# Seven Strassen products in place of four tiles for the output of token block 7

## Chip, cores and metric

The kernel runs on one core of a Trainium2 chip. The metric is the device time of one execution in microseconds (us), the median of several runs. The profile is of one further execution; its span is counted from the first to the last instruction that the profiler saw.

## What is computed

Eight batches, eight heads, 576 rows of 64 values. Keys and values are averaged over groups of 8 rows, attention is a softmax over the 72 averaged keys, and the heads' results, put side by side, make x of 4608 tokens by 512. Then a maxout layer with three weights and an output weight:

```
k_p, v_p = means of k, v over groups of 8 rows
x = softmax(q @ k_p.T / 8) @ v_p            # 4608 x 512
h = max(x @ w1, x @ w2, x @ w3)             # 4608 x 768
out = h @ w_out                             # 4608 x 512, float32
```

## The kernel before

The kernel subtracts w1 from w2 and w3 once (`sub_w`), so that h = x@w1 + max(0, x@(w2-w1), x@(w3-w1)). The first part goes straight through to the output by a weight `wm` = w1@w_out. The output of a token is therefore one sum over 512 + 768 = 1280 rows: `xT` against `wm` (4 slices of 128 rows) and the maxout value `hT` against `wo_sb` (6 slices).

The 4608 tokens are cut into nine blocks of 512, numbered 0 to 8. Blocks 0 to 5 get their maxout values by plain matmuls (`hidden`, L346). Blocks 6 to 8 get them by seven Strassen products (`seven`): the sums of activations T1 to T4 are made by `fold_x` (`fold_t`, L598), those of weights beforehand, and each product is done for three groups of rows, a, b and c (L733, 4 matmuls of 256 columns each). ScalarE copies products out of PSUM (L739, L743), VectorE adds others (L711) and takes the maximum (`best`, L714), which writes rows of `hT`: the group's row g with product 3, its row g+3 with product 4.

The output of a block is done in one of two ways. `project` takes four tiles of 128 tokens; a tile is 4 matmuls of 512 columns with `wm` (L391) and 6 with `wo_sb` (L395) into one PSUM bank, a copy by ScalarE (L400) and two stores of 128 KB by SyncE's queue (L404). `out_seven` does a block by seven Strassen products over 256 columns: each product is 5 matmuls for each of two halves m of 128 tokens (L670). Its sums come from three places: of weights from `fold_out`, 20 GpSimd subtractions and additions handed out one by one between the products (L628), of x from `fold_x` again, of maxout values from `fold_h`. Before the change only block 8 goes this way.

The three Strassen blocks run in `weave`, where the program order of every engine is written out by hand in the string `ORDER`. `1a` is product 1 of group a of the next block that has not had it (so the first is block 6's, the third block 8's); `T` is `fold_x` of the next block; `F` is half a tile of `project`; `s70` is a piece of batch 7's scores and `v62` chunk 2 of batch 6's attention output, which VectorE normalises and a DMA transpose on SyncE's queue (L239) puts into `xT`; `k7` is batch 7's keys. After `weave` come the remaining half tiles, `out_seven` of block 8 in the order 1 1 2 2 6 6 7 5 5 7 3 3 4 4, and as the very last work one tile cut into two halves of 256 columns, so that the end has short copies and stores.

PSUM in this stage: tags `pa` (2 banks) for products 1, 6, 5, 3, `sc` (2) and `bc` (1) for products 2 and 7/4, `po` (1) for tiles, `val` (2 banks, one buffer) for attention output.

Of the kernel before, what the change touches and what calls it, by code (L numbers as in the profile page):

```python
# [10 lines left out]
ALU = mybir.AluOpType  # L11
# [3 lines left out]
def kernel(  # L15
# [11 lines left out]
    nc = tc.nc  # L27
# [14 lines left out]
    NG = 9  # L42
# [338 lines left out]
    def project(n):  # L381
        hT = hTs[n]
        for mm in range(4):
            m = 4 * n + mm
            last = m == TOK // 128 - 5
            osb = sb3.tile([128, C], F32, name="osb", tag="osb", bufs=5)
            for c in ((slice(0, C // 2), slice(C // 2, C)) if last else (slice(0, C),)):
                tag = PW if len(pools) < 3 else (PO, SC, PA)[max(0, m - (TOK // 128 - 7))]
                po = psum([128, c.stop - c.start], F32, name="po", tag=tag[0], bufs=tag[1])
                for kc in range(KCH):  # L390
                    nc.tensor.matmul(po, xT[:, kc, bass.ts(m, 128)], wm_sb[:, kc, c],  # L391
                                     start=(kc == 0), stop=False)
                yield
                for jc in (0, 3, 1, 4, 2, 5):
                    nc.tensor.matmul(po, hT[:, jc, bass.ts(mm, 128)], wo_sb[:, jc, c],  # L395
                                     start=False, stop=(jc == JCH - 1))
                if c.start:
                    nc.vector.tensor_copy(out=osb[:, c], in_=po)
                else:
                    nc.scalar.copy(out=osb[:, c], in_=po)  # L400
                for u in range(2):
                    b, g = divmod(2 * m + u, NG)
                    dst = out[S * b:S * b + S, :].rearrange("(r g) c -> r g c", g=NG)
                    (nc.scalar if last and u else nc.sync).dma_start(  # L404
                        out=dst[:, GS[g], c], in_=osb[64 * u:64 * u + 64, c])
            yield
# [186 lines left out]
    def turns(n):  # L593
        return (pad3 if n % 2 else pad)[:, 0:4]

    def fold_t(e, x, t):
        for i, a, b in ((0, x[1], x[0]), (1, x[3], t[0]), (2, x[3], x[1]), (3, x[2], t[1])):
            e.tensor_tensor(out=t[i], in0=a, in1=b, op=ALU.subtract)  # L598

    def fold_x(n):  # L600

        x, t = halves(n), turns(n)
        for part in ([slice(0, 1), slice(1, 2)] if n == LAST else [slice(0, 2)]):
            fold_t(nc.gpsimd if n == LAST else nc.vector,
                   {i: x[i][:, part] for i in x}, [t[:, i, part] for i in range(4)])
        return {f"T{i + 1}": t[:, i] for i in range(4)}

# [22 lines left out]

    def fold_h(n):

        th[n] = ld.tile([128, 4, JH, HALF], F16, name="th", tag="ktFalse")
        h = {i: hTs[n][:, JH * (i // 2):JH * (i // 2) + JH,
                       HALF * (i % 2):HALF * (i % 2) + HALF] for i in range(4)}
        fold_t(nc.vector, h, [th[n][:, i] for i in range(4)])

    def out_seven(n):

        o = sb2.tile([128, 2304], F32, name="ob", tag="et")[:, 0:2048].rearrange(  # L640
            "p (j m c) -> p j m c", j=2, m=2)
        lo, hi = slice(0, HALF), slice(HALF, C)
        banks, done = {}, set()

        def store(e, j, c):
            for u in range(2):
                b, g = divmod(2 * (4 * n + 2 * j) + u, NG)
                dst = out[S * b:S * b + S, :].rearrange("(r g) c -> r g c", g=NG)
                e.dma_start(out=dst[:, GS[g]:GS[g + 2] + 1:4, c],
                            in_=o[64 * u:64 * u + 64, j, :, c])  # L650

        def product(i, m):
            of = "B" if i == 2 else "C" if i in (4, 7) else "A"
            if i in FIRST:
                tag = {"A": PA, "B": SC, "C": BC if m == 0 else SC}[of]
                banks[of, m] = psum([128, 2, HALF], F32, name=f"o{of}", tag=tag[0],
                                    bufs=tag[1])
            p = banks[of, m][:, 0]
            za, zb = PRODUCTS[i]
            for r in range(5):  # L660
                c = slice(128 * m, 128 * m + 128)
                if isinstance(zb, str):
                    z = int(zb[1]) - 1
                    left = turns(n)[:, z, r, c] if r < 2 else th[n][:, z, r - 2, c]
                else:
                    at = HALF * (zb % 2) + 128 * m
                    left = (xT[:, 2 * (zb // 2) + r, NB * n + at:NB * n + at + 128] if r < 2
                            else hTs[n][:, JH * (zb // 2) + r - 2, at:at + 128])
                right = out_s(int(za[1]))[:, r] if isinstance(za, str) else out_w(za, r)
                nc.tensor.matmul(p, left, right, start=(i in FIRST and r == 0), stop=(r == 4),  # L670
                                 skip_group_check=True)
            done.add((i, m))

            def copy(j, c):
                nc.scalar.copy(out=o[:, j, m, c], in_=p)

            def plus(j, c, p):
                nc.vector.tensor_tensor(out=o[:, j, m, c], in0=o[:, j, m, c], in1=p,
                                        op=ALU.add)

            if i in (1, 5, 6, 3):
                copy(i in (5, 3), lo if i in (1, 3) else hi)
            elif i == 2:
                plus(0, lo, p)
                if m:
                    store(nc.gpsimd, 0, lo)
            elif i == 4:
                plus(0, hi, p)
                if m:
                    store(nc.sync, 0, hi)  # L690
            if i in (5, 7) and (12 - i, m) in done:
                plus(1, hi, banks["C", m][:, 0])
            if i in (5, 7, 3) and all((z, m) in done for z in (5, 7, 3) for m in range(2)):
                store(nc.sync, 1, slice(0, C))

        return product

    def seven(n):
# [19 lines left out]
        def product(i, g):  # L718
            if i == 0:
                x.update(fold_x(n))  # L720
                return
            if not done:
                hTs[n] = new_hT()
            of = "B" if i == 2 else "C" if i in (4, 7) else "A"
            if i in FIRST:
                tag = {"A": PA, "B": SC, "C": BC}[of]
                banks[of, g] = psum([128, 2, HALF], F32, name=f"p{of}", tag=tag[0],
                                    bufs=tag[1])
            p = banks[of, g]
            for w in range(2):  # L730
                a, b = sw[w + 1][PRODUCTS[i][0]], x[PRODUCTS[i][1]]
                for kc in range(2):
                    mm = nc.tensor.matmul(p[:, w], a[:, kc, bass.ts(g, 128)], b[:, kc, :],  # L733
                                          start=(i in FIRST and w + kc == 0),
                                          stop=(w + kc == 2), skip_group_check=True)
            mms.append(mm)
            done.add((i, g))
            if i in (1, 6, 5):
                nc.scalar.copy(out=kept(i, g), in_=p)  # L739
            if i == 2:  # L740
                plus(top(g)[:, 0], 1, g, p)
            elif i == 3:
                nc.scalar.copy(out=top(g)[:, 1], in_=p)  # L743
                best(g, top(g))
            elif i == 4:
                plus(low[:, 0], 6, g, p)
                best(g + JH, low)
            elif i in (5, 7) and (12 - i, g) in done:
                plus(low[:, 1], 5, g, banks["C", g])
# [1 line left out]
        return product  # L751

    ORDER = """
        k7 F F T v62 1a 1b F s70 s71 6a 6b 2a 7a s72 v63 5a s73 F 2b 5b 4a s74 3a
        s75 F s76 7b 1c s77 v64 s78 4b 6c F v70 2c 5c 7c 3b F v71 3c F 4c 1a 1b T F
        v72 2b F 2a 6b 6a 7a F v73 5a F v74 3a 5b 4a F 1c F 6c 7b 3b T F 5c 4b F 7c
        1a 2c 2a 4c 6a 3c F 5a 7a 1b 2b 3a 6b 4a 1c 2c 5b 6c 7b 3b F 4b 5c F 7c 3c F
        4c
    """

    def weave():

        products, seen, sums = {}, {}, fold_out()
        for name in ORDER.split():
            if name == "F":
                next(tiles)
            elif name[0] in "ksvx":
                b = int(name[1])
                do(b, name[0] + name[2:])
# [20 lines left out]
    for n in range(2, 5):  # L790
# [8 lines left out]
    stage.close()  # L799
    pools.append(ctx.enter_context(tc.tile_pool(name="psq", bufs=1, space=PSUM,  # L800
                                                reuse_waits="tile")))
    tiles = (t for n in range(5, LAST) for t in project(n))
    weave()
    next(tiles)
    next(tiles)
    outs = out_seven(LAST)
    fold_h(LAST)
    for i, m in ((1, 0), (1, 1), (2, 0), (2, 1), (6, 0), (6, 1), (7, 0), (5, 0), (5, 1),
# [34 lines left out]
```

The softmax here doesn't subtract the row's maximum and nothing guards it: scores larger than these inputs give would overflow.

## Time and profile before

| what | before |
|---|---|
| time, median of 3 | 231.08 us (230.59 to 231.42) |
| span of the profiled execution | 229.0 us |
| TensorE busy | 219.8 us (96%) |
| VectorE busy | 130.5 us (57%) |
| ScalarE busy | 122.6 us (54%) |
| GpSimd busy | 140.0 us (61%) |
| a Strassen product of L733 (4 matmuls) | 0.44 us in the chain |
| a tile: L391 and L395 | 0.86 + 1.29 us in the chain |
| a product of `out_seven`, both halves (10 matmuls) | 1.09 us in the chain |
| VectorE: L711 / L714 | 685 / 810 ns mean, 18 each after 160 us |
| ScalarE: L739, L743 / L400 | 587, 584 / 585 ns |
| GpSimd sum of 128x256: L628, L598 | 668 to 921 ns by form |

The profile is read as follows. The chain of waits follows the work back from the last instruction: where it stays on one engine, that engine was never waiting, and its work sets the time. The windows give the busy time of every engine in a stretch. The timeline gives instructions in order of time with the idle time before them and what ended it. "xT<-xn" means that the instruction writes tile xT from tile xn.

### The profile page before, as it was taken

To read this page: it belongs to the slowest core of one execution; us is meant where nothing else is said; L and a number is where in the kernel's file an instruction comes from. 1 tells how busy PE (TensorE), PEld (TensorE's weight loads), DVE (VectorE), ACT (ScalarE), POOL (GpSimd) and SP (SyncE) were. 2 spreads that over 40 slices of the span, in tenths; PEclk is the share of its full clock that TensorE was granted. 3 is DMA by queue.
4 is the path that set the end of the run, shared out by engine and by line. 5 is a ranking of instruction groups with operands and counts; after the bars stand their busy time and mean duration, and the time that the engine had idled before them with its cause. 6 is when DMAs were issued, how large, how long until landed. Compare 5 with 4: busy or idle time off the path is not lost.

```text
span 229.0 us, 4411 instructions
## 1 busy us (share of the span) xinstructions
PE 219.8 (96%) x1686; PEld 134.9 (59%) x1687; DVE 130.5 (57%) x246; ACT 122.6 (54%) x221; POOL 140.0 (61%) x115
## 2 busy tenths in 40 slices
PE   7888999999999999999999999999999999999992
PEld 2477645568655545544554455455677667786682
DVE  3668876048426423632363236368578887897830
ACT  2277425756864586238623852683776435465330
POOL 7975201999959999999999759900343443920020
PEclk9999999999999999999999999999999999999999
DMA  6999999999569999986998799941421534301326
GB/s 172 208 197 197 211 202 208 194 177 225 106 110 216 221 161 212 159 194 119 223 153 199 127 218 189 190 110 24 92 53 40 121 71 87 84 11 46 76 68 183
DMA packets 47157, 33.52 MB, mean 146 GB/s; under 512 B 27104, under 2 KB 41888, under 8 KB 47136
## 3 DMA queue, kind: packets, MB, share of 16 engines
q0 software_dynamic: 16944, 16.98, 46.0%
q1 hardware_dynamic: 30032, 16.13, 32.2%
q8 instruction: 13, 0.21, 0.4%
q10 hardware_dynamic: 160, 0.13, 0.2%
q14 instruction: 8, 0.07, 0.1%
HBM read 34.60 MB, written 9.44 MB: 192 GB/s over the span
## 4 chain that ended last, share of the span: by engine, by line
PE 88%; DVE 6%; ACT 3%; issue 2%; DVEq 0%; ACTq 0%
PE pw L346 23%; PE po L395 18%; PE po L391 11%; PE pA L733 7%; PE psc L207 6%; PE pav L255 4%; PE pC L733 3%; PE wm L413 3%; PE pm L333 2%; PE oA L670 2%; PE pB L733 2%; DVE kz L198 2%; PE pqt L182 2%; DVE xn L263 2%; ACT kz L198 2%
## 5 line engine op out<-in xcount | busy, mean ns | idle before, releaser
L346 PE MATMUL pw<-xT,mw 128*128 128x512 f16 (+1 forms) x336 | 73.1, 349 | 0.4 <-ACT xT L249 0.2
L395 PE MATMUL po<-mwo,hT 128*128 128x512 f16 (+1 forms) x198 | 46.8, 373 | 0.0
L354 DVE TENSOR_TENSOR hT<-t,pw 128x512 f16<-128x512 f16 (+1 forms) x42 | 25.5, 610 | 36.7 <-ACT et L212 22.3
L346 PEld LDWEIGHTS <-mw 128*128 128x128 f16 x336 | 31.6, 98 | 21.5 <-DVE mw L319 0.6
L400 ACT COPY osb<-po 128x512 f32<-128x512 f32 (+1 forms) x32 | 18.5, 579 | 41.2 <-PE po L395 41.1
L212 ACT ACTIVATE et<-psc 72x576 f16<-72x576 f32 (+2 forms) x54 | 35.2, 660 | 7.1 <-PE psc L207 6.9
L151 POOL TENSOR_TENSOR half<-vt 72x2048 f32<-72x2048 f16 x7 | 28.4, 4060 | 14.1 <-DMA vt<-in_v_dram 13.7
L391 PE MATMUL po<-wm,xT 128*128 128x512 f16 (+1 forms) x132 | 33.0, 372 | 0.3 <-ACT osb L400 0.3
L352 ACT ACTIVATE t<-pw 128x512 f16<-128x512 f32 (+1 forms) x42 | 22.5, 537 | 13.4 <-PE pw L346 11.6
L263 DVE TENSOR_TENSOR xn<-pav,rcp 128x512 f16<-128x512 f32 x40 | 27.7, 691 | 1.6 <-DVE rcp L261 0.2
L395 PEld LDWEIGHTS <-hT 128*128 128x128 f16 x198 | 18.5, 98 | 16.3
L152 POOL TENSOR_TENSOR half<-half 72x1024 f32<-72x1024 f32 (+1 forms) x13 | 27.3, 2097 | 1.0
L207 PE MATMUL psc<-qT,kz 128*128 128x320 bf16 (+2 forms) x120 | 22.9, 278 | 1.8 <-DVE qT L184 0.9
L207 PEld LDWEIGHTS <-kz 128*128 128x128 bf16 x143 | 13.1, 98 | 14.7 <-ACT kz L198 2.0
L151 POOL TENSOR_TENSOR half<-ktFalse 96x1536 f32<-96x1536 f16 x6 | 18.6, 3099 | 4.3 <-DMA ktFalse<-in_k_dram 4.1
L255 PEld LDWEIGHTS <-et 72*128 72x128 f16 x320 | 15.4, 98 | 7.6 <-issue 0.3
L739 ACT CAST pad<-pA 128x512 f16<-128x512 f32 x27 | 15.3, 587 | 8.4 <-PE pA L733 6.0
L261 DVE RECIPROCAL rcp<-pav 128x8 f32<-128x8 f32 x40 | 8.2, 206 | 18.1 <-PE pav L255 17.9
L391 PEld LDWEIGHTS <-xT 128*128 128x128 f16 x132 | 12.1, 98 | 9.4 <-issue 0.4
L255 PE MATMUL pav<-vp,et 72*128 72x65 f16 x320 | 17.0, 194 | 0.1
L714 DVE SCALAR_TENSOR_TENSOR hT<-pad 128x512 f16<-128x512 f16 x18 | 14.4, 810 | 1.8 <-ACT pad L743 1.4
L733 PEld LDWEIGHTS <-sw 128*128 128x128 f16 x144 | 13.7, 98 | 2.7
(106 smaller groups left out, 279.2 us busy)
## 6 DMA issues: line engine op xcount, KB each, us to landing
out_dram<-osb SPq DMA_DIRECT2D x62, 128.0 KB, 3.2
ktFalse<-in_k_dram POOLq DMA_DIRECT2D x7, 576.0 KB, 6.6
qb<-in_q_dram POOLq DMA_DIRECT2D x7, 576.0 KB, 13.2
vt<-in_v_dram POOLq DMA_DIRECT2D x7, 576.0 KB, 10.9
mw<-in_moe_w_dram POOLq DMA_DIRECT2D x9, 256.0 KB, 9.2
ktTrue<-in_k_dram SPq DMA_DIRECT2D x3, 384.0 KB, 5.0
mwo<-in_moe_w_out_dram POOLq DMA_DIRECT2D x1, 768.0 KB, 13.2
qb<-in_q_dram POOLq DMA_DIRECT2D x2, 288.0 KB, 7.8
```

The costliest lines, as they stand in the source:

```text
L151: e.tensor_tensor(out=f, in0=t[:, :, 0:4, :], in1=t[:, :, 4:8, :], op=ALU.add)
L152: e.tensor_tensor(out=f[:, :, 0:2, :], in0=f[:, :, 0:2, :], in1=f[:, :, 2:4, :], op=ALU.add)
L207: nc.tensor.matmul(out, kz_all[b % 2][f % 2][:, h, :], qTs[b][:, n + i0:n + i1, 64 * (h % 2):64 * (h % 2) + 64], start=True, stop=True)
L212: nc.scalar.activation(out=out, in_=in_, func=FT.Exp, scale=1.0 / 64.0)
L255: nc.tensor.matmul(pav[:, h // 4, 65 * (h % 4):65 * (h % 4) + 65], ets[b][:, h, c0:c0 + 128], vp_all[:, b, h, :], start=True, stop=True)
L263: nc.vector.tensor_tensor(out=xn, in0=pv[:, :, :, 0:D], in1=rcp.to_broadcast([128, 2, 4, D]), op=ALU.mult)
L346: mm = nc.tensor.matmul(pw, w_sb[wi][:, kc, bass.ts(jc, 128)], xT[:, kc, col], start=(kc == 0), stop=(kc == KCH - 1))
L352: nc.scalar.activation(out=t, in_=pw, func=FT.Relu)
L354: nc.vector.tensor_tensor(out=hT[:, jc, c0:c1], in0=t, in1=pw, op=ALU.max)
L391: nc.tensor.matmul(po, xT[:, kc, bass.ts(m, 128)], wm_sb[:, kc, c], start=(kc == 0), stop=False)
L395: nc.tensor.matmul(po, hT[:, jc, bass.ts(mm, 128)], wo_sb[:, jc, c], start=False, stop=(jc == JCH - 1))
L733: mm = nc.tensor.matmul(p[:, w], a[:, kc, bass.ts(g, 128)], b[:, kc, :], start=(i in FIRST and w + kc == 0), stop=(w + kc == 2), skip_grou ...
```

## The change

Block 7's output goes by seven Strassen products too, and these stand in `ORDER` among block 8's maxout products, which the tiles of block 7 had stood among. Of the parts:

- `project` runs for blocks 5 and 6 only. The tile that is kept for the very end is now block 6's last (m = 27), again cut in two; the other tiles all use `po`.
- `fold_x` of block 7 moves from VectorE (4 operations of 128x512) to GpSimd (8 of 128x256), as block 8's already was.
- `H` in `ORDER` is the new `fold_h` of block 7: T1 and T2 of the maxout values for the first two rows on VectorE, the third row of these and all of T3 and T4 on GpSimd, row by row, each as its rows of `hT` come.
- `o1` to `o7` are the products of block 7's output, both halves m in one PSUM bank, taken out by one operation of 512 values where block 8 takes two of 256.
- `store` writes two rows of groups by one DMA where their place in the output allows it, and by two where not.
- `hT` of block 8 and the sums of `fold_h` get other buffers, since `hT` of block 6 now lives to the end.
- `ORDER` is written anew for all three blocks.

The core of the diff:

```diff
-            last = m == TOK // 128 - 5
+            last = m == TOK // 128 - 9
-                tag = PW if len(pools) < 3 else (PO, SC, PA)[max(0, m - (TOK // 128 - 7))]
+                tag = PW if len(pools) < 3 else PA if last else PO
...
-        for part in ([slice(0, 1), slice(1, 2)] if n == LAST else [slice(0, 2)]):
-            fold_t(nc.gpsimd if n == LAST else nc.vector,
+        late = n >= LAST - 1
+        for part in ([slice(0, 1), slice(1, 2)] if late else [slice(0, 2)]):
+            fold_t(nc.gpsimd if late else nc.vector,
...
+        if n < LAST:
+            t = ld.tile([128, 4, JH, HALF], F16, name="th", tag="ktFalse")
+            th[n] = [t[:, i] for i in range(4)]
+
+            def part(e, which, r0, r1):
+                for i in which:
+                    a, b = ((h[1], h[0]), (h[3], t[:, 0]), (h[3], h[1]), (h[2], t[:, 1]))[i]
+                    e.tensor_tensor(out=t[:, i, r0:r1], in0=a[:, r0:r1], in1=b[:, r0:r1],
+                                    op=ALU.subtract)
+
+            part(nc.vector, (0, 1), 0, JH - 1)
+            for r in (JH - 1, 0, 1):
+                part(nc.gpsimd, (0, 1) if r == JH - 1 else (2, 3), r, r + 1)
+            part(nc.gpsimd, (2, 3), JH - 1, JH)
+            return
...
     ORDER = """
-        k7 F F T v62 1a 1b F s70 s71 6a 6b 2a 7a s72 v63 5a s73 F 2b 5b 4a s74 3a
-        s75 F s76 7b 1c s77 v64 s78 4b 6c F v70 2c 5c 7c 3b F v71 3c F 4c 1a 1b T F
-        v72 2b F 2a 6b 6a 7a F v73 5a F v74 3a 5b 4a F 1c F 6c 7b 3b T F 5c 4b F 7c
-        1a 2c 2a 4c 6a 3c F 5a 7a 1b 2b 3a 6b 4a 1c 2c 5b 6c 7b 3b F 4b 5c F 7c 3c F
-        4c
+        k7 1a F F 2a T 1b v62 s70 F s71 s72 6a F s73 v63 5a 7a s74 s75 v64 F s76 4a
+        s77 3a s78 6b 2b 7b 1c v70 2c 5b T F 6c v71 3b F 5c 4b F v72 7c 3c 1a F 1b
+        4c v73 2a 2b 6b 6a F v74 5a 7a F 3a F T 1c 4a 5b 2c 6c 7b 3b F 5c 4b F 1a 7c
+        2a 3c 6a 4c H 1b 2b 5a 6b 7a 3a o1 1c 4a o2 5b 6c 7b 2c o6 4b 3b 5c o5 7c o7
+        4c 3c o3 o4
     """
...
+            elif name == "H":
+                fold_h(LAST - 1)
+                outs = out_seven(LAST - 1)
+            elif name[0] == "o":
+                outs(int(name[1]), 0, 1)
...
-    tiles = (t for n in range(5, LAST) for t in project(n))
+    tiles = (t for n in range(5, LAST - 1) for t in project(n))
     weave()
-    next(tiles)
-    next(tiles)
```

More of the change, by code (lines that the diff above doesn't have):

```diff
@@ L631, in fold_h @@
     def fold_h(n):
-        th[n] = ld.tile([128, 4, JH, HALF], F16, name="th", tag="ktFalse")
         h = {i: hTs[n][:, JH * (i // 2):JH * (i // 2) + JH,
                        HALF * (i % 2):HALF * (i % 2) + HALF] for i in range(4)}
-        fold_t(nc.vector, h, [th[n][:, i] for i in range(4)])
+        if n < LAST:
[11 more added lines that the diff above has]
+            return
+        u = [ld.tile([128, 9, HALF], F16, name="th2", tag="qb"),
+             sb2.tile([128, 9, HALF], F16, name="th4", tag="qT")]
+        th[n] = [u[i // 2][:, JH * (i % 2):JH * (i % 2) + JH] for i in range(4)]
+        fold_t(nc.vector, h, th[n])
     def out_seven(n):
@@ L647, in store, with bank, product, matmuls @@
                 b, g = divmod(2 * (4 * n + 2 * j) + u, NG)
[L648 to L654, printed above, removed]
+                pair = g + 2 < NG and GS[g + 2] == GS[g] + 4
+                for m in range(0, 2, 1 + pair):
+                    b, g = divmod(2 * (4 * n + 2 * j + m) + u, NG)
+                    dst = out[S * b:S * b + S, :].rearrange("(r g) c -> r g c", g=NG)
+                    e.dma_start(out=dst[:, GS[g]:GS[g] + 4 * pair + 1:4, c],
+                                in_=o[64 * u:64 * u + 64, j, m:m + 1 + pair, c])
+        def bank(of, m):
+            if n < LAST:
+                if of not in banks:
+                    if of == "A":
+                        banks["A"] = psum([128, 2, 2, HALF], F32, name="oA", tag="val",
+                                          bufs=1)[:, 0]
+                    else:
+                        tag = (PO, SC)[of == "C"]
+                        banks[of] = psum([128, 2, HALF], F32, name=f"o{of}", tag=tag[0],
+                                         bufs=tag[1])
+                return banks[of]
+            if (of, m) not in banks:
                 tag = {"A": PA, "B": SC, "C": BC if m == 0 else SC}[of]
                 banks[of, m] = psum([128, 2, HALF], F32, name=f"o{of}", tag=tag[0],
-                                    bufs=tag[1])
-            p = banks[of, m][:, 0]
+                                    bufs=tag[1])[:, 0:1]
+            return banks[of, m]
+        def product(i, *ms):
+            for m in ms:
+                matmuls(i, m)
+            done.update((i, m) for m in ms)
+            evict(i, ms)
+        def matmuls(i, m):
+            of = "B" if i == 2 else "C" if i in (4, 7) else "A"
+            p = bank(of, m)[:, m if n < LAST else 0]
             za, zb = PRODUCTS[i]
@@ L663, in product @@
                     z = int(zb[1]) - 1
-                    left = turns(n)[:, z, r, c] if r < 2 else th[n][:, z, r - 2, c]
+                    left = turns(n)[:, z, r, c] if r < 2 else th[n][z][:, r - 2, c]
                 else:
@@ L669, in product, with evict, plus, ended @@
                 right = out_s(int(za[1]))[:, r] if isinstance(za, str) else out_w(za, r)
-                nc.tensor.matmul(p, left, right, start=(i in FIRST and r == 0), stop=(r == 4),
-                                 skip_group_check=True)
-            done.add((i, m))
-            def copy(j, c):
[L675 to L679, printed above, removed]
+                nc.tensor.matmul(
+                    p, left, right, stop=(r == 4), skip_group_check=True,
+                    start=(i in FIRST and r == 0 and (m == 0 or n == LAST)))
+        def evict(i, ms):
+            m, at = ms[0], slice(ms[0], ms[-1] + 1)
+            def copy(j, c):
+                nc.scalar.copy(out=o[:, j, at, c], in_=bank("A", m))
+            def plus(j, c, of):
+                nc.vector.tensor_tensor(out=o[:, j, at, c], in0=o[:, j, at, c],
+                                        in1=bank(of, m), op=ALU.add)
+            def ended(*parts):
+                return all((z, k) in done for z in parts for k in range(2))
             if i in (1, 5, 6, 3):
-                copy(i in (5, 3), lo if i in (1, 3) else hi)
+                copy(int(i in (5, 3)), lo if i in (1, 3) else hi)
             elif i == 2:
-                plus(0, lo, p)
-                if m:
-                    store(nc.gpsimd, 0, lo)
+                plus(0, lo, "B")
             elif i == 4:
-                plus(0, hi, p)
-                if m:
-                    store(nc.sync, 0, hi)
+                plus(0, hi, "C")
             if i in (5, 7) and (12 - i, m) in done:
-                plus(1, hi, banks["C", m][:, 0])
-            if i in (5, 7, 3) and all((z, m) in done for z in (5, 7, 3) for m in range(2)):
+                plus(1, hi, "C")
+            if i in (5, 7, 3) and ended(5, 7, 3):
                 store(nc.sync, 1, slice(0, C))
+            if n == LAST and i in (2, 4) and ended(i):
+                store((nc.gpsimd, nc.sync)[i // 4], 0, (lo, hi)[i // 4])
+            if n < LAST and i in (2, 4) and ended(2, 4):
+                store(nc.sync, 0, slice(0, C))
         return product
@@ L722, in product @@
             if not done:
-                hTs[n] = new_hT()
+                hTs[n] = (ld.tile([128, JCH, NB], F16, name="hT8", tag="ktFalse")
+                          if n == LAST else new_hT())
             of = "B" if i == 2 else "C" if i in (4, 7) else "A"
```

## The prediction

> **What bounds the kernel now.** I read the page's slices first, then the busy times by stretch, then the chain of waits, and last the timeline at the places that the change touches.
>
> ```profile
> span 229.0 us, 4411 instructions
> PE   7888999999999999999999999999999999999992
> POOL 7975201999959999999999759900343443920020
> ...
> 160.00:165.00 5.00, 4.73 (x40) 3.14 (x39) 3.40 (x9) 3.40 (x7) 0.98 (x2) 1.00 0.33 70
> 195.00:200.00 5.00, 5.00 (x41) 3.72 (x39) 3.91 (x6) 1.99 (x4) 4.84 (x7) 1.00 0.34 77
> 205.00:210.00 5.00, 5.00 (x39) 3.60 (x38) 4.25 (x8) 3.30 (x6) 0.00 (x0) 1.00 0.00 0
> ...
> 162.80 0.04 issue
> 162.84 1.02 PE po L391 x4
> ...
> 211.18 1.29 PE po L395 x6
> 212.47 0.44 PE pC L733 x4
> 212.91 0.86 PE po L391 x4
> 213.77 1.29 PE po L395 x6
> 215.07 1.09 PE oA L670 x10
> ```
>
> The stretch rows give PE, PEld, DVE, ACT and POOL busy time in that order. In the stage of the change, 159 to 225 us, TensorE has no gap but one at 162.8 (behind a ScalarE copy), and the chain stays on it, item after item. So this stage lasts as long as TensorE's work plus its waits. VectorE has about a fifth of its time free, GpSimd most of it except around block 8's `fold_x`. The end is a tail of a copy and stores after the last matmul:
>
> ```profile
> 222.05 2.91 SPq L649 DMA_DIRECT2D out_dram<-ob  x4
> 224.24 1.63 ACTq L404 DMA_DIRECT2D out_dram<-osb  x2
> 224.93 0.42 DVE L398 COPY osb<-po 128x256 f32<-128x256 f32 x1 [1.76 <-PE po L395]
> 225.05 1.33 SPq L404 DMA_DIRECT2D out_dram<-osb  x2
> ```
>
> From the last matmul (224.91) to the end of the span it is 4.1 us. The tail belongs to block 8's stores and the split tile.
>
> **What the Trainium skill says.** "TensorE: Matmul & The Clock Gate", section Back-to-back issue gap, gives about N/2.4 + 2.5 ns for a warm matmul of N columns, 109 ns for 256; the chain's 1.09 us for ten agrees. "SBUF — State Buffer", section Who interferes with whom, says that a VectorE operation with two SBUF inputs and a GpSimd operation that reads SBUF exclude each other for the whole instruction, whichever starts first, while a VectorE operation with one SBUF input is left alone. The trace agrees:
>
> ```profile
> 181.82 0.96 POOL L628 TENSOR_TENSOR so<-mwo,so 128x256 f16<-128x256 f16 x1 [0.27 <-PE pA L733]
> 182.17 0.89 DVE L598 TENSOR_TENSOR pad<-xT 128x512 f16<-128x512 f16 x1
> 182.74 0.84 POOL L628 TENSOR_TENSOR so<-mwo 128x256 f16<-128x256 f16 x1
> 183.09 0.77 DVE L598 TENSOR_TENSOR pad<-xT,pad 128x512 f16<-128x512 f16 x1
> 183.79 0.41 DVE L598 TENSOR_TENSOR pad<-xT 128x512 f16<-128x512 f16 x1
> ```
>
> The reader is to see the same VectorE subtraction at 0.89 and 0.77 us beside GpSimd and 0.41 alone, and GpSimd's own at 0.96 and 0.84 instead of 0.67. `best` (two SBUF inputs) ranges from 0.69 alone to 1.18 beside GpSimd, mean 0.81; the addition from PSUM (one) keeps 0.685. "Perfetto Trace Analysis", section GPSIMD Engine Instruction, advises timing GpSimd by the spacing of starts: block 8's eight operations plus the start after them go from 194.88 to 200.92, so 0.755 us each, which I use.
>
> **TensorE's work.** Removed are block 7's four tiles: 4 x (0.86 + 1.29) = 8.60 us. Added are 7 products of 1.09 = 7.63 us. Net -0.97 us. Nothing else on TensorE changes in amount: 63 maxout products, scores and values stay, and the sum of the others is only put in another order. Since the chain lies wholly on TensorE here, all of this counts unless waits come in.
>
> **The tail.** It stays: block 8's products in the same order, then a split tile with the same copies and queues (27 for 31). Block 7's last stores, 1 MB in six issues, start about when block 8's output does and have 7 us before the next store of 222.05 is due, at some 250 GB/s (the mean of the last stretch) about 4 us. So I count 0.
>
> **The old wait at 162.8.** The third F waits for ScalarE's copy of the tile before it, as there is one `po` bank; the copy stands behind two key copies that end at 162.18. TensorE could have gone on at 162.41 (two products end), so 0.43 us are lost. In the new order `1a` goes ahead of the tile, and its ScalarE copy too. The copy of the tile is then at 162.20 + 0.48 (the spacing of such copies) to 163.26, the F at 163.32; by TensorE's own sum (0.13 k7, 0.44, 2.15 tile, 0.87, 0.26 v62, 0.22 s70 after 158.99) it would be there at 163.07. The wait becomes 0.25; gain 0.18 us.
>
> **GpSimd's new work.** Sixteen more operations, 16 x 0.755 = 12.1 us, in a queue that runs in order. I add up TensorE's items in the new order by the chain's durations (product 0.437, halves of a tile 0.864 and 1.295, s 0.22, v 0.265, o 1.09) from k7 at 158.99, and 0.25 for the third F. That puts v70 at about 172.5, v74 at 185.8, 6a of block 7 at 184.1, 6a of block 8 at 197.3, `H` at 199.8 when 4c's value is there (below), o6 at 205.7 and o7 at 209.6. From v to the landed transpose it took 4.0 us beyond its 0.27 (189.13 to 193.4: pav, rcp, xn, 1.2 and 2.4 us for the transpose). So block 7's `fold_x` starts at 176.8 and T2 (sixth operation) is there at 181.3, 2.8 us early. Block 8's starts at 190.0, T2 at 194.6, 2.7 us early. Five sums follow to 199.8, then `H`: T2's third row at 201.4 (needed at 205.7), T3's last, the seventh, at 205.1 (needed at 209.6). Queued behind are only later sums with the same slack. So GpSimd holds nobody: 0. Its mean would have to be over 0.97 us to be late at o7.
>
> **VectorE.** It loses block 7's `fold_x` (2.48 us with its conflicts), and gets two operations of `H` (0.41 each) and three additions of 512 values (about 0.69). Net +0.4 us in 55 us; it has some 13 free. But the place matters: `H`'s two stand right after block 7's last `best`, ahead of 2b and 7a of block 8, and 4a must wait until VectorE has taken 7a out of their common bank. From the start of k7, by TensorE's sum: 3c ends 38.14; ScalarE's copy to 38.77; `best` to 39.4; 4c's addition (4c ends 39.02) to 40.0; `best` to 40.6; `H` to 41.4; 2b's addition to 42.0; 7a's to 42.7; 4a is due at 43.17. That is 0.45 us of slack with nothing in the way. GpSimd is however busy all through: five sums, then its part of `H`. The trace's `best` beside a steadily busy GpSimd (195 to 203 us) cost 0.16 more on average, two of them 0.33; the two of `H` cost 0 to 0.83 more (0.41 to 0.89 and 0.77); I take half, 0.4. Sum 0.73, less 0.45 slack: a wait of 0.3 us. Ends: 0, and 0.9 with two `best` at 0.25 each and the full 0.83. Behind 4a all of TensorE waits, so it counts whole.
>
> Elsewhere the walk showed no wait: `best`'s higher price on blocks 6 and 7 falls where tiles and values stand between products. At the end (same count) 3c's `best` is done at 54.0, after o7's and 4c's operations, and block 8's first product reads that row at 55.0; block 8's `fold_h`, queued behind o4's addition, has T2 at 56.3, and product 6 reads it at 56.95. The three additions and four copies of the `o` are read by stores alone, or by the next `o` of their bank over 1 us later. New buffers were last read long before. The bank of the first `1a`, which now comes 2.4 us earlier in a freshly opened PSUM pool, is not shown by the trace: 0 if its old tenant is read out, up to 1.1 us if it is the last `hidden` bank (read until 160.24, `1a` due at 159.12). I take 0, since k7 and the tile found free banks there.
>
> **Sum.** -0.97 - 0.18 + 0.3 = -0.85 us: 231.08 becomes 230.2 us.
>
> **Rivals.**
> - All hidden: the conflict with GpSimd falls elsewhere, no wait at 4a. -1.15: 229.9 us. For it speaks that some `best` beside GpSimd kept 0.70. Chance 0.10.
> - VectorE becomes the bound around `H`: wait 0.9 or several smaller ones. -0.25: 230.8 us, not to be told from no change. For it speaks that VectorE's slack is under half a microsecond there; against it, that the worst prices must all meet. Chance 0.24.
> - Slower: the opening bank (1.1) and 4a (0.9) together, -1.15 + 2.0 = +0.85: 231.9 us. Or GpSimd at 1.12 us each, its dearest here: T3 at 190.0 + 20 x 1.12 = 212.4, 2.8 late at o7, +1.65: 232.7 us. Against both: only single operations cost that. Chance 0.16.
> - The forecast: 0.50.
>
> **How the numbers follow.** Faster by over 0.3% means below 230.39: the forecast and all hidden, 0.60; within: 0.24; slower: 0.16. The range goes from all hidden less 0.3 for the spread of runs (229.6) to just under the slower case (231.7).
>
> **What would show it.** The last matmul 0.8 to 0.9 us earlier against the span's end unchanged at 4.1 us; no idle TensorE but at the third F (0.25) and before 4a of block 8 (0.3, released by VectorE's L711); GpSimd nearly without gap from 177 to 206 us; o6 and o7 not waiting for GpSimd. A wait of TensorE on GpSimd, a first `1a` late, or a longer tail would prove me wrong.

## The result and the profile after

The changed kernel takes 231.68 us (six runs, 231.40 to 232.16) against 230.72 for the kernel before on the same chip: ratio 1.0041, 95% interval 1.0022 to 1.0060. Run again with more runs (experiment a_again) it is 231.33 against 230.79, ratio 1.0021, interval 1.0010 to 1.0031. It is slower by half a microsecond to one, where 0.85 us less were forecast.

The page and the stretches of the changed kernel. The stretch rows give PE, PEld, DVE, ACT and POOL busy time, then the clock, the DMA share and GB/s:

```profile
span 230.1 us, 4490 instructions
PE   7788999999999999999999999999999999989992
POOL 7975200999949999999999829920125987992020
```

```profile
160.00:165.00 5.00, 4.90 (x38) 2.93 (x37) 3.25 (x8) 3.01 (x6) 1.34 (x2) 1.00 0.13 26
195.00:200.00 5.00, 5.00 (x42) 3.88 (x41) 3.81 (x6) 2.93 (x6) 4.84 (x7) 1.00 0.25 56
200.00:205.00 5.00, 4.03 (x37) 3.44 (x36) 4.85 (x8) 2.97 (x6) 4.92 (x7) 1.00 0.00 0
205.00:210.00 5.00, 5.00 (x48) 4.48 (x47) 4.07 (x7) 1.97 (x4) 3.29 (x5) 1.00 0.00 0
```

TensorE has a new gap of a microsecond at 200 to 205 us, where VectorE and GpSimd are both full. The chain of waits, which never left TensorE there before, now goes through VectorE:

```profile
200.31 0.04 DVE hT L760
...
201.31 0.90 DVE th L643
...
202.93 1.28 DVE pad L757 x2
204.21 0.04 issue
204.25 0.60 PE pC L780 x4
```

L643 is `H`, L757 the additions of 2b and 7a of block 8, L780 its product 4a. The tail after the last matmul (225.60):

```profile
224.94 1.62 ACTq L404 DMA_DIRECT2D out_dram<-osb  x2
225.63 0.42 DVE L398 COPY osb<-po 128x256 f32<-128x256 f32 x1 [1.76 <-PE po L395]
225.74 1.33 SPq L404 DMA_DIRECT2D out_dram<-osb  x2
```

These are issued just as before against the last matmul, yet the span ends 4.5 us after it and not 4.1.

To account for the time I cut each trace in three: up to k7's first matmul (nothing before it is changed), from there to the last matmul ("stage"), and the tail. Microseconds; the ratio is to the kernel before on the same chip.

| kernel | time | ratio, interval | k7 | stage | tail |
|---|---|---|---|---|---|
| before | 230.72 | | 158.99 | 65.92 | 4.09 |
| b_again | 230.80 | 0.9998 (0.9982-1.0013) | 159.13 | 65.92 | 4.05 |
| after | 231.68 | 1.0041 (1.0022-1.0060) | 159.71 | 65.90 | 4.49 |
| a_again | 231.33 | 1.0021 (1.0010-1.0031) | 159.03 | 65.88 | 4.49 |
| h_late | 230.47 | 0.9985 (0.9976-0.9995) | 158.88 | 64.99 | 4.53 |
| sums_early | 230.69 | 0.9993 (0.9984-1.0001) | 159.00 | 65.25 | 4.45 |
| h_sums | 230.37 | 0.9980 (0.9967-0.9993) | 159.12 | 64.75 | 4.53 |
| h_x7_dve | 232.01 | 1.0040 (1.0026-1.0054) | 159.08 | 66.56 | 4.46 |
| h_swap | 230.49 | 0.9984 (0.9971-0.9997) | 160.21 | 64.99 | 4.40 |
| b_tile28 | 230.81 | 1.0003 (0.9990-1.0016) | 159.30 | 65.92 | 4.08 |
| act_shift | 230.16 | 0.9966 (0.9953-0.9979) | 159.52 | 64.76 | 4.22 |
| sp_shift | 230.32 | 0.9976 (0.9965-0.9988) | 158.99 | 64.75 | 4.66 |
| b_less | 233.30 | 1.0118 (1.0091-1.0145) | 159.31 | 65.92 | 6.37 |
| best | 230.09 | 0.9963 (0.9949-0.9978) | 159.09 | 64.66 | 4.55 |
| a_act | 231.17 | 1.0009 (0.9999-1.0020) | 159.21 | 65.94 | 4.25 |
| b_fetch | 231.35 | 1.0015 (0.9999-1.0030) | 158.80 | 66.49 | 4.11 |
| best_act | 229.83 | 0.9958 (0.9944-0.9972) | 159.25 | 64.64 | 4.21 |

The stage repeats to 0.02 us between traces of one kernel, the tail to 0.04 (it is taken from a span given to 0.1 us, so it is good to some 0.05). k7's start does not (158.8 to 160.2 in kernels whose code is the same up to it); a single span says little here, the two other columns much. The change left the stage where it was (-0.04) and made the tail 0.42 longer.

### The profile page after: what moved, and what is told of

The parts are those of the page before. It is cut to its first block, busy times and chain, and to the rows that moved or that the text cites. A ratio compares the mean times of both kernels' runs of the same rounds, so it can differ in the third digit from the quotient of the medians.

```text
span 230.1 us, 4490 instructions
## 1 busy us (share of the span) xinstructions
PE 218.9 (95%) x1717; PEld 137.4 (60%) x1717; DVE 130.9 (57%) x247; ACT 122.4 (53%) x221; POOL 153.5 (67%) x131
## 4 chain that ended last, share of the span: by engine, by line
PE 83%; DVE 5%; DMA 4%; ACT 3%; issue 2%; POOL 1%; DVEq 0%; ACTq 0%; POOLq 0%
PE pw L346 24%; PE po L395 16%; PE po L391 10%; PE pA L780 6%; PE psc L207 5%; PE pav L255 4%; DMA vt<-in_v_dram 4%; PE oA L710 3%; PE pC L780 3%; PE pm L333 2%; PE oC L710 2%; PE pB L780 2%; PE pxt L245 1%; DVE kz L198 1%; ACT kz L198 1%
## 5 line engine op out<-in xcount | busy, mean ns | idle before, releaser
L395 PE MATMUL po<-mwo,hT 128*128 128x512 f16 (+1 forms) x174 | 41.0, 371 | 0.0
L400 ACT COPY osb<-po 128x512 f32<-128x512 f32 (+1 forms) x28 | 16.2, 579 | 35.9 <-PE po L395 30.5
L391 PE MATMUL po<-wm,xT 128*128 128x512 f16 (+1 forms) x116 | 28.9, 371 | 0.1
L395 PEld LDWEIGHTS <-hT 128*128 128x128 f16 x174 | 16.1, 98 | 14.1
L391 PEld LDWEIGHTS <-xT 128*128 128x128 f16 x116 | 10.5, 98 | 8.2 <-issue 0.2
L760 DVE SCALAR_TENSOR_TENSOR hT<-pad 128x512 f16<-128x512 f16 x18 | 14.3, 806 | 1.7 <-ACT pad L790 1.3
L198 DVE COPY kz<-pkt 64x288 bf16<-64x288 bf16 x18 | 8.7, 481 | 11.4 <-PE pkt L189 11.2
```

## Experiments

**The two kernels again.** Both unchanged. For b_again:

> The kernel before, unchanged, for a second profile. First theory: the 0.7 us by which the changed kernel's trace is late before the changed stage begins (the first matmul of k7 at 159.7 against 159.0 us) and the 0.4 us by which its tail is longer are chance of single executions; then k7 starts anywhere between 158.7 and 159.9 here and the tail after the last matmul is 4.1 to 4.5. Rival: they belong to the change; then k7 is at 159.0 and the tail 4.1 again. Time 230.7 us either way.

For a_again:

> The changed kernel, unchanged, for a second profile. Chance: k7 nearer to 159.2 or scattered, tail 4.1 to 4.5. Rival: k7 at 159.7 and tail 4.5 again. Both: TensorE's wait before 4a of block 8 is 1.0 us again. Time 231.7 us.

k7 at 159.13 and 159.03: its 0.7 us in the first trace were chance. The tails, 4.05 and 4.49, were not: the first theory holds for the start and falls for the tail. The wait before 4a is there again. The timeline of VectorE (first fence) and of GpSimd (second) around it in a_again, start and duration in us:

```profile
198.91 0.68 DVE L757 TENSOR_TENSOR pad<-pad,pC 128x512 f16<-128x512 f16 x1
199.62 1.07 DVE L760 SCALAR_TENSOR_TENSOR hT<-pad 128x512 f16<-128x512 f16 x1
200.61 0.89 DVE L643 TENSOR_TENSOR th<-hT 128x512 f16<-128x512 f16 x1
201.53 0.77 DVE L643 TENSOR_TENSOR th<-hT,th 128x512 f16<-128x512 f16 x1
202.23 0.68 DVE L757 TENSOR_TENSOR pad<-pad,pB 128x512 f16<-128x512 f16 x1
202.83 0.67 DVE L757 TENSOR_TENSOR pad<-pad,pC 128x512 f16<-128x512 f16 x1
```

```profile
199.48 0.66 POOL L629 TENSOR_TENSOR so<-mwo 128x256 f16<-128x256 f16 x1
200.10 1.11 POOL L629 TENSOR_TENSOR so<-mwo,so 128x256 f16<-128x256 f16 x1
201.18 0.85 POOL L643 TENSOR_TENSOR th<-hT 128x256 f16<-128x256 f16 x1
202.10 0.73 POOL L643 TENSOR_TENSOR th<-hT,th 128x256 f16<-128x256 f16 x1
```

VectorE never stands still, and each of its operations with two SBUF inputs (L760, L643) is drawn out, as GpSimd's are in turn, while its additions from PSUM (L757) keep 0.68. TensorE's side of it:

```profile
201.99 0.60 PE L780 MATMUL pA<-xT,mw 128*128 128x256 f16 x4
203.56 0.60 PE L780 MATMUL pC<-pad,mw 128*128 128x256 f16 x4 [0.96 <-DVE pad L757]
```

The product before 4a takes its 0.44 us to 202.43, so 1.13 us are lost (the row's 0.96 counts from the modelled end of the matmuls).

**h_late.**

```diff
-        2a 3c 6a 4c H 1b 2b 5a 6b 7a 3a o1 1c 4a ...
+        2a 3c 6a 4c 1b 2b 5a 6b 7a H 3a o1 1c 4a ...
```

> The changed kernel with H four products later, after 7a of block 8, so that VectorE takes 2b and 7a before the sums of maxout values. Theory: the wait of 1.0 us before 4a was VectorE's queue order alone; it goes, and the time is 230.7 us (-1.0). Rival: VectorE (or GpSimd, whose part of H now starts later) is the bound there, and the wait only moves to the next product or to o6; 231.4 to 231.7 us.

230.47 us; stage -0.89. The wait before 4a is gone; 0.2 us come back before 4b of block 8, where VectorE's addition of 7b is late. So the order of VectorE's queue was the wait's cause, and the rival falls.

**sums_early.** The other way at the same wait.

```diff
-                if n < LAST and len(mms) % 2:
+                if n < LAST:
                     next(sums, None)
```

> The changed kernel with the 20 sums of output weights handed out after every product and not after every second, so that none of them stands on GpSimd between block 8's T and H. Theory that conflicts with GpSimd made the wait: best of 4c falls from 1.07 to about 0.7 us and the first operation of H from 0.89 to about 0.41, the wait before 4a from 1.0 to about 0.2, the time to 230.9 us. Rival, the order alone: the wait stays at 0.7 or more, 231.4 to 231.7 us.

VectorE at the place, with GpSimd idle until 199.26 but for block 8's T:

```profile
199.81 0.69 DVE L760 SCALAR_TENSOR_TENSOR hT<-pad 128x512 f16<-128x512 f16 x1
200.42 0.42 DVE L643 TENSOR_TENSOR th<-hT 128x512 f16<-128x512 f16 x1
200.87 0.77 DVE L643 TENSOR_TENSOR th<-hT,th 128x512 f16<-128x512 f16 x1
```

The last `best` falls from 1.07 to 0.69 and the first of `H` from 0.89 to 0.42, as expected; the second still meets GpSimd's own part of `H`. The wait before 4a is 0.22 us (202.68 to 202.90), 0.91 less, but the stage only -0.63: the sums now stand beside block 6's `fold_x` on VectorE (0.62 and 0.78 us there for 0.41), and its product 6a waits 0.28 us, to 164.91. Order and conflict are both needed for the wait: either taken away, it nearly goes.

**h_sums.** h_late, and the condition `len(mms) % 2 or seen.get("5a")`.

> H late as in h_late, and the sums of output weights after every second product until 5a of block 6 and after every product from there, so that GpSimd has none between block 8's T and H. Theory: both changes act on the same wait before 4a of block 8, which is already gone, so little is left: 0 to -0.2 us against h_late's 230.47 (the 0.2 us before 4b of block 8). Rival, conflicts of GpSimd with VectorE cost TensorE at more places than this one: -0.4 us or more, 230.1 or less.

Stage -0.24 against h_late, no wait of TensorE left but at the third F; time -0.1. The theory's size.

**h_x7_dve.** h_late, with block 7's `fold_x` on VectorE again.

```diff
-        late = n >= LAST - 1
+        late = n == LAST
```

> H late as in h_late, with fold_x of block 7 back on VectorE (4 operations of 128x512). Theory: GpSimd's fold_x hid behind other work and gave VectorE 2.5 us back in a stretch where VectorE is not the bound; without it the time is the same within 0.3 us of h_late's 230.47. Rival: VectorE has no room near v71 to v73 and TensorE waits, +0.5 to +1.5 us.

232.01 us, stage +1.57: the rival's wait. VectorE, whose queue is in order, stands before this `fold_x` until the transposes of x have landed, and TensorE then waits for what is queued behind:

```profile
176.87 0.43 DVE L598 TENSOR_TENSOR pad<-xT 128x512 f16<-128x512 f16 x1 [1.59 <-POOL so L629]
```

```profile
179.80 0.43 PE L255 MATMUL pav<-vp,et 72*128 72x65 f16 x8 [0.40 <-DVE xn L263]
...
181.00 0.60 PE L780 MATMUL pC<-pad,sw 128*128 128x256 f16 x4 [0.76 <-DVE pad L757]
```

(The chain names the landing of xT<-xn, at 176.46, as what ended VectorE's 1.59 us; the releaser in the row had long been done.) So the move to GpSimd carries this order, not because VectorE lacked time but because GpSimd can stand waiting without holding anybody.

**The tail: where the last stores land.** h_swap on h_late, b_tile28 on the kernel before.

In h_swap, with the like for tile 31 in `out_seven`'s `store`:

```diff
-                    b, g = divmod(2 * m + u, NG)
+                    b, g = divmod(2 * m + u + 8 * last, NG)
```

> H late as in h_late; the last tile (27) stores its rows at tile 31's place in the output and block 7's tile 31 at tile 27's, so the output has these rows exchanged. Theory that the longer tail comes from where the last stores land (tile 27: both halves in one batch, 4 KB apart; tile 31: two batches): the tail after the last matmul falls from 4.5 to about 4.1 us and the time to 230.1 us. Rival, it comes from the stores before it or from chance of the queue: tail stays at 4.5, time 230.5 us.

In b_tile28, where the place in the order, and not m, then says which tile is split and which bank it takes:

```diff
-        for mm in range(4):
+        for k, mm in enumerate((1, 2, 3, 0) if n == TOK // NB - 2 else range(4)):
```

> The kernel before, with block 7's tiles in the order 29, 30, 31, 28, so that the last tile's two halves land in one batch, 4 KB apart, as tile 27's do. Theory of the landing place: tail 4.5 us in place of 4.1, time 231.2 us (+0.4). Rival: tail 4.1 and 230.8 us.

Tails of 4.40 and 4.08: the place in the output has nothing to do with it. That theory fell.

**The tail: a fetch of instructions.** The DMA queues carry more than data: the Trainium skill, "Runtime: NRT & Kernel Launch", section Instruction fetch mechanics, says that each engine's sequencer fetches its program through a DMA queue of its own while it runs, and calls the cost mostly hidden. The traces show such fetches, and here one that is not hidden. The DMA queues in the stretch 222 to 223 us of the kernel before, and in 226.5 to 227.5 of a_again (queue, kind: packets, MB, share of 16 engines):

```profile
q14 instruction: 1, 0.01, 3.0%
```

```profile
q1 hardware_dynamic: 235, 0.19, 61.0%
q14 instruction: 1, 0.01, 1.9%
```

By the time of its packet (8 KB) it starts 2.23 us before the last matmul's end in the former, ahead of most of the last stores, and 1.85 after it in the latter (and in every trace of a changed kernel up to here), one packet of 0.31 us amid the last stores. In a_again the last store's sixteenth completion comes 3.37 us after the last matmul, behind fifteen that are in by 3.09; before, all are in by 3.12.

In act_shift (on h_sums):

```diff
-                    nc.scalar.copy(out=osb[:, c], in_=po)
+                    for h in ((slice(0, C // 2), slice(C // 2, C)) if 20 < m < 27 else (c,)):
+                        nc.scalar.copy(out=osb[:, h], in_=po[:, h] if h != c else po)
```

> h_sums with ScalarE's copies of tiles 21 to 26 in two halves each: six more instructions on ScalarE, 0.16 us more of its time each. In all traces of the changed kernels an 8 KB fetch of instructions starts 1.85 us after the last matmul, in the kernel before 2.2 us ahead of it; in the changed ones the last two stores have one of 16 engines late by 0.3 us. Theory: that fetch lies among the last stores and makes the tail 4.5 in place of 4.1 us, and it is ScalarE's program that comes to its boundary there; then it moves ahead here, the tail is 4.1 and the time 230.0 us. Rivals: it is SyncE's program (fetch and tail as before, 230.4 us), or the fetch moves and the tail stays 4.5 (no cause).

In sp_shift (on h_sums):

```diff
+                    for h in ((slice(0, C // 2), slice(C // 2, C)) if m in (25, 26) else (c,)):
...
-                pair = g + 2 < NG and GS[g + 2] == GS[g] + 4
+                pair = n == LAST and g + 2 < NG and GS[g + 2] == GS[g] + 4
```

> h_sums with six more stores on SyncE's queue, of the same bytes: tiles 25 and 26 in halves of columns, block 7's stores one row of groups each. Theory that the fetch in the tail is SyncE's program: it moves ahead of the last matmul, tail 4.1, time 230.0 us. Rival that it is ScalarE's: fetch at +1.85 and tail 4.5 again, 230.4 us.

act_shift: the fetch comes 10.8 us before the last matmul's end, the last completion at 3.09, the tail 4.22. sp_shift: fetch at +1.88, tail 4.66. So it is not SyncE's program; it is ScalarE's, and with the fetch away from the last stores most of the longer tail is gone.

The changed kernel itself with act_shift's edit alone:

> The changed kernel itself, H at its place, with ScalarE's copies of tiles 21 to 26 in two halves (six more instructions of ScalarE). If the place of ScalarE's 8 KB instruction fetch is the second cause of the change's loss and adds to the first: fetch ahead of the last matmul, tail 4.1 to 4.2, the wait of 1.1 us before 4a as it was, 231.0 us (-0.3 against the changed kernel). If the two are bound together in another way: tail 4.5, 231.3 us.

In the changed kernel itself: fetch at -10.55, last completion 3.09, tail 4.25, stage 65.94, 231.17 us (ratio 1.0009 for 1.0021). So the two causes add up. The medians bear the gain out less sharply than the traces: by the ratios 0.28 us for a_act against a_again and 0.32 for act_shift against h_sums, with intervals of 0.2 to 0.3 us to either side, but only 0.16 between the medians of act_shift and sp_shift, whose tails differ by 0.44. SyncE's wait for its last store, from the waits of a_again and of a_act:

```profile
SPq L888 <- DMA out_dram<-osb: 1.5, 1, 1.5
```

```profile
SPq L889 <- DMA out_dram<-osb: 1.2, 1, 1.2
```

The fetch explains 0.28 of the 0.42 us, from 3.09 to 3.37. The rest lies in SyncE's closing waits. At the end SyncE waits for eight semaphores of its DMAs (the counts that tell of their landing) one after the other, in the same order in all 17 traces. In the kernel before, the store that lands last belongs to the seventh of the eight, in the changed kernel to the fifth, so two more waits follow upon its landing. SyncE's waits from the landing of the last store on, before (from 228.04) and in a_again (from 228.29); the row gives their number, ns of one, and first and last start:

```profile
L838 SPq EVENT_SEMAPHORE  x2: 28/28/28, 228.1 to 228.1; - x2
```

```profile
L888 SPq EVENT_SEMAPHORE  x4: 28/28/28, 228.3 to 228.5; - x4
```

They start 0.06 us apart. From the landing to the instruction behind them it is 0.15 us before and 0.28 in the changed kernel, in act_shift and in a_act; from there on every trace takes 0.84 or 0.85 us more. So 0.13 us stay when the fetch is away. In h_swap and sp_shift the last store's semaphore is the sixth and the third, and it is 0.20 and 0.39 us: hence their tails of 4.40 and 4.66.

The kernel before, with the fetch pushed the other way:

In b_less:

```diff
-                for u in range(2):
+                for u in range(0 if m in (24, 25) else 2):
```

> The kernel before without the stores of tiles 24 and 25 (their rows of the output are not written): four instructions fewer or more on SyncE's queue, TensorE's work the same. If the fetch is SyncE's, it moves from 2.2 us ahead of the last matmul into the tail, and the tail grows from 4.1 to about 4.5, the time to 231.2 us. If ScalarE's, fetch, tail and time stay (230.8 us).

In b_fetch:

```diff
-                if c.start:
+                if c.start or m in (22, 24, 26, 28):
```

> The kernel before with the copies of tiles 22, 24, 26 and 28 on VectorE: four instructions fewer on ScalarE. By the theory of the fetch it moves from 2.2 us ahead of the last matmul into the tail, which becomes 4.4 us or longer, the time 231.2 us or more, with TensorE's stage near 65.9 us. Rival: the fetch alone costs nothing there; tail 4.1.

Neither gave the tail that was expected. In b_less the fetch came at +1.65, into the last stores, and the tail became 6.37, because one of ScalarE's two store issues took 3.99 us where it takes 0.56 in the kernel before (ScalarE's queue, both issues together):

```profile
224.56 4.63 ACTq L404 DMA_DIRECT2D out_dram<-osb  x2
```

The fetch moved there although it isn't SyncE's. With the stores two records of ScalarE's queue are gone from the trace, 326 for 328, and over all 17 traces the fetch's place goes by this number: with 330 records it starts 10.5 to 10.8 us before the last matmul's end, with 328 2.0 to 2.2 before, with 326 1.65 after, with 324 1.85 to 1.9 after, with 322 3.14 after. It does not go by SyncE's: with 176 records it is at +1.85 in a_again and at -10.8 in act_shift. In b_fetch the fetch went past the last stores, to +3.14, and the tail is 4.11: there it harms nobody. The stage grew by 0.57, nearly all of it one wait of TensorE at 186.43 us; the four copies now stand in VectorE's queue. So in the kernel before no fetch was put where it costs just 0.3 us; that it costs this rests on the changed kernels.

**best and best_act.** The opening reordered, so that the wait at the third F goes:

```diff
-        k7 1a F F 2a T 1b v62 s70 F s71 ...
+        k7 F F 1a T 2a 1b v62 s70 F s71 ...
```

> sp_shift with the opening in the order k7 F F 1a T 2a 1b, so that ScalarE copies the first tile before product 1a and VectorE's fold_x of block 6 stands ahead of 2a's addition. Theory: the wait of 0.3 us at the third F goes, -0.3 us against sp_shift: 229.7 us if the tail is short there, 230.1 if not. Rival: the wait moves to s71 or 6a, time as sp_shift.

> All that was found put together: H late, sums after every product from 5a on, the opening in the order k7 F F 1a T 2a 1b, ScalarE's copies of tiles 21 to 26 in halves. Sum of the parts: stage 64.6, tail 4.2, 229.8 us. If the six more instructions cost TensorE a wait or the fetch falls badly: 230.1 us or more.

best: the wait at the third F is gone (160 to 165 us has no idle TensorE), and the time is 0.23 us below sp_shift's, but the stage only 0.09 of a wait of 0.25. Half of it, 0.12, came back inside the third F, whose first four matmuls take 0.99 us from start to start (163.17 to 164.16) for 0.86 (163.36 to 164.22) in a_again. best_act: 229.83 us, ratio 0.9958 (0.9944 to 0.9972), 1.0 us faster than the kernel before and 1.5 than the changed one: the wait at 4a and the fetch in the tail are gone, and TensorE shows no gap:

```profile
160.00:165.00 5.00, 5.00 (x43) 3.28 (x42) 4.63 (x10) 3.28 (x7) 2.14 (x3) 1.00 0.27 59
200.00:205.00 5.00, 5.00 (x48) 4.47 (x47) 4.91 (x9) 2.97 (x6) 3.66 (x5) 1.00 0.00 0
205.00:210.00 5.00, 5.00 (x48) 4.49 (x47) 3.72 (x6) 2.93 (x6) 1.64 (x3) 1.00 0.00 0
```

## Why the prediction was wrong

- *TensorE's work, -0.97.* Right. The stage of h_sums, with the third F's wait as its only one, is 1.17 under the kernel before's, 1.15 being forecast for the case without a wait at 4a.
- *The old wait, 0.43 to 0.25.* Right: in a_again the third F starts at 163.36 in place of 163.11 (the sum's 163.07, from a k7 that is 0.04 later), 0.25.
- *GpSimd holds nobody.* Right. Block 7's `fold_x` starts at 176.5 (said 176.8), and TensorE waits for GpSimd nowhere. Its spacing was 0.81 to 0.84 and not 0.755.
- *The wait at 4a: "Sum 0.73, less 0.45 slack: a wait of 0.3 us."* The mechanism and the place were right, the size failed: 1.13, beyond the upper end of 0.9. From 3c's start to the end of 7a's addition VectorE took 6.56 us (196.94 to 203.50) where the sum without conflicts had 5.0. Spacing of starts against the prices used: the last `best` 0.99 for 0.61, the two of `H` 0.92 and 0.70 for 0.41, the `best` before 0.66 for 0.61; together 1.23 of conflict, for which 0.73 was put in. The rest, 0.33, is the way from a matmul through ScalarE to VectorE (1.31 us from 3c's start to its `best`, counted as 1.10) and 0.1 us in the spacing of the additions; this ate most of the slack of 0.45. The dearest case had allowed 1.33 of conflict, so it is this longer way that took the wait beyond 0.9. GpSimd was busy without a break there; by "SBUF — State Buffer", section Who interferes with whom, which these rows bear out, such an operation and one of GpSimd's that reads SBUF exclude each other. Three of the four on VectorE waited; at the fourth (0.66) it was GpSimd's that took 1.00 us. The full price was the likely one, not half of it.
- *The tail: "So I count 0."* This step failed by +0.42. Block 7's stores did not reach into it: the last of them landed 4.25 us before the last matmul's end. The count looked at data only. ScalarE's program is a little shorter by the trace (324 records of its queue for 328), and one of its fetches moved from before the last stores into their midst, 0.28; and the last store's place among SyncE's closing waits changed, 0.13.
- *Sum.* -0.97 - 0.18 + 1.13 + 0.42 = +0.40, against +0.54 in the longer measurement (ratio 1.0021, interval 0.2 to 0.7 us) and +0.96 in the first, of six runs. That the range, which ended at 231.7, held both times was luck: direction and size were wrong, by two terms of which the forecast had one too small and the other not at all.

What stays open: why the first measurement came out 0.4 us above the second; why six more instructions on ScalarE bring its fetch more than 12 us ahead; and why a store's issue took 3.99 us in b_less.

## What to carry to other kernels

A part moved off the busiest engine is paid for in the queues of the others: give every helper operation its place by who is queued behind it, and where a GpSimd that reads SBUF runs without a break, price each VectorE operation with two SBUF inputs at its dearest, not at its mean. Cut traces at points that both versions share before comparing them: here the stage repeated to 0.02 us while the start of the stage scattered by over one. And an effect under half a microsecond at a kernel's end can come from instruction traffic that a change of a few instructions moves; look at every kind of DMA in the tail, and at the order in which its landings are waited for.

## What the runs showed of the hardware

- ScalarE's instructions come by DMA in pieces of 8 KB, on a queue (q14) that the profile counts among the same 16 DMA engines as the data. One such fetch of 0.31 us among the last stores goes with one of the sixteen completions of the last store at 3.37 us after the last matmul and not at 3.09. In b_less, with the fetch at +1.65, an issue of a store on ScalarE's queue lasted 3.99 us for 0.56. Six more instructions on ScalarE brought the fetch 12.4 to 12.6 us ahead.
- SyncE's closing waits run one after the other, 0.06 us each: how many stand behind the one for the store that lands last made 0.08 (b_less, none) to 0.39 us (sp_shift, five).
- VectorE and GpSimd hold each other up in both directions: beside each other in a_again VectorE's 0.41 became 0.89 and 0.77, and GpSimd's 0.67 became 1.11, within two microseconds.
